# Squared-ReLU attention feeding a conv-gated FFN on one core: the FFN starts one block later, and the weight preparation is spread wider

## The chip, the cores and the metric

The kernel runs on one core of one Trainium2 chip. The metric is the device time of one execution in microseconds (us); lower is better. Three runs of the kernel before gave 1623.33, 1624.53 and 1624.59 us, so its time is the median, 1624.53 us.

## What is computed

```python
scores = (z @ z.T) / S                      # per batch, S = 3136, z is [S, 64]
x = u * (np.maximum(scores, 0) ** 2 @ v)    # u, v: [4, 3136, 256]
h = np.maximum(x @ w_in, 0)                 # w_in: [256, 1024]
conv = conv_w[0]*h[t-1] + conv_w[1]*h[t] + conv_w[2]*h[t+1]   # along the sequence
out = (h * sigmoid(conv)) @ w_out           # w_out: [1024, 256]
```

The three weight arrays arrive as float64; the rest is float32.

## The kernel before, in words

**Blocks and slots.** The queries are cut into 28 blocks (4 batches of 7) of 448 columns. A block goes over the 3136 keys of its batch in 25 slots, one per tile of 128 keys; the last tile is half a tile. So there are 700 slots. What each engine is to do in slot k stands in a table `ev[k]`, in six classes (PRE, MID, VEC, POST, PE0, PE1), and the loop at the end of the kernel walks the slots and issues each class in turn. Every engine carries out its own instructions in the order in which they were issued.

**Attention.** In slot k the kernel issues `attend(k)` (six matmuls: two halves dc of the output, three products each because values are split in a high and a low part; four matmuls in the half tile), and ahead of it `scores(k+4)` (two matmuls), `relu(k+3)` on ACT with `square(k+3)` on DVE, and `split_hi(k+2)` on ACT with `split_lo(k+2)` on DVE. Since z z^T is symmetric, some tiles are not computed again: POOL packs a computed tile (`part`), a DMA spills it to DRAM, and later blocks fetch it transposed (`fetch`, `join`); such a slot needs no scores and no square. The attention of one block is summed in two PSUM tiles `av0` and `av1`, one buffer each.

**From block to block.** At the first slot of block b+1, in class PRE, `gate_x` reads both `av` tiles of block b (DVE line L348 the first, ACT line L352 the second) and multiplies by u. The first attend matmul of block b+1 (L337) writes `av0` again and so waits for L348. One slot later `split_x` makes `xh` and `xl` (ACT L360, POOL) for the FFN.

**FFN.** The 1024 hidden columns of a block are eight chunks of 128. A chunk that starts in slot s issues `ffn_in` (six matmuls, L370 to L372, in class PE1, after attend and scores) in slot s, the ReLU in s+1, tap and first convolution step in s+2, the second step in s+3, sigmoid and gating in s+4, the split in s+5, and `ffn_out` (three matmuls each, L437 to L439, in class PE0, ahead of attend) in slots s+10 and s+11. Chunk f of block b starts at slot 25(b+1) + FS[f].

**Weights.** Each of the 16 blocks of 128x256 weights (eight of `w_in`, eight of `w_out`) is loaded as float64 words and rebuilt in float32 by `prep_w`, in five stages spread over four slots that start at WS[i]: two DVE instructions (L205, L209), two ACT and two DVE instructions (L216, L220), a POOL product (L222), a copy and a POOL subtraction. I call this one **weight set**. The three convolution weights go through the same stages once, starting in slot 5.

**Names in the rows.** `s`: scores in PSUM; `t`: ReLU output; `ah`, `al`: attention tile, high and low; `vh`, `vl`: values; `wr`, `wm`: raw and half-made weights; `ph`: FFN hidden tile in PSUM; `gh`, `gl`: gated hidden tile; `o`: FFN output in PSUM; `pl`, `tp`, `tj`: packed, fetched and joined tiles.

The line that sets the slots of the FFN before, and the one that reads it:

```python
FS = [2, 5, 8, 11, 15, 18, 21, 24]
...
            s = k0 + FS[f]          # k0 = (blk + 1) * NJ, NJ = 25
```

Of the kernel before, what the change touches and what calls it, by code (L numbers as in the profile page):

```python
# [8 lines left out]
F32 = mybir.dt.float32  # L9
F32R = mybir.dt.float32r  # L10
# [19 lines left out]
LD, LJ, LP, LX = 9, 5, 2, 1  # L30


FS = [2, 5, 8, 11, 15, 18, 21, 24]
RELU, TAP, ST1, ST2, SIG, GATE, GHI, OUT0, OUT1 = 1, 2, 2, 3, 4, 4, 5, 10, 11
EVAC = 12
XS = 1
# [2 lines left out]
C_RELU, C_TAP, C_XS, C_EV, C_V = 3, 1, 3, 3, 5  # L39


WS = [0, 8, 11, 17, 15, 21, 27, 22, 29, 34, 36, 38, 40, 45, 48, 53]
WST = [0, 1, 1, 2, 3]
W_E = ["GGGGGGGGGVGGGGGG", "AVVAAAAAVAAAAAAA"]
W_C = 5
# [11 lines left out]
def kernel(  # L57
# [11 lines left out]
    B, S, D = v.shape  # L69
# [3 lines left out]
    P = 128  # L73
    NB = 448
    QB = S // NB
    NJ = (S + P - 1) // P
    HALF = S - (NJ - 1) * P
    NBLK = B * QB
    NS = NBLK * NJ
    DC = D // P  # L80
    FC = DFF // P
# [5 lines left out]
    wk = ctx.enter_context(tc.tile_pool(name="wk", bufs=2))  # L87
# [15 lines left out]
    def at_slot(k):  # L103
        blk, i = divmod(k, NJ)
        return blk, *ent[blk % QB][i]
# [13 lines left out]
    def sub(eng, out, a, b):  # L119
        eng.tensor_tensor(out=out, in0=a, in1=b.bitcast(F32), op=ALU.subtract)  # L120
# [61 lines left out]
        return r[:, :, 0], r[:, :, 1]  # L182

    def load_w(what, i):
        t = wk.tile([P, 2 * D], F32, tag="wr", name="wr", bufs=3)
        raw = t.bitcast(U64)
        if what == "in":
            nc.sync.dma_start(
                out=raw.rearrange("p (a n) -> p a n", a=DC),
                in_=w_in[:, i * P : (i + 1) * P].rearrange("(a p) n -> p a n", p=P),  # L190
            )
        else:
            nc.sync.dma_start(out=raw, in_=w_out[i * P : (i + 1) * P, :])
        wst[what, i] = [t]
# [50 lines left out]
    def scores(k):  # L245
        blk, j, tr = at_slot(k)
        if tr:
            return

        tag = "ph" if k < NJ and k % 2 else "s"  # L250
        s = ps.tile([P, 512], F32, tag=tag, name="s", bufs=2)
        w = slice(j * P, (j + 1) * P)
        nc.tensor.matmul(s[:, :NB], lhsT=zhh[:, w], rhs=zq[blk], start=True, stop=False)  # L253
        nc.tensor.matmul(s[:, :NB], lhsT=zll[:, w], rhs=zq[blk], start=False, stop=True)  # L254
        sc[k] = s
# [88 lines left out]
    xh, xl = {}, {}  # L344
# [9 lines left out]

    def split_x(blk, engs):
        t = ut.pop(blk)
        xh[blk] = wk.tile([P, DC, NB], F32R, tag="xh", name="xh", bufs=1)
        xl[blk] = wk.tile([P, DC, NB], F32R, tag="xl", name="xl", bufs=1)
        for dc in range(DC):
            nc.scalar.copy(xh[blk][:, dc], t[:, dc])  # L360
            sub(engs[dc], xl[blk][:, dc], t[:, dc], xh[blk][:, dc])


    ph, hb, cc, gg, po = {}, {}, {}, {}, {}
# [13 lines left out]
    def width(blk):  # L378
        return NB + (2 if blk % QB == QB - 1 else 0)
# [63 lines left out]
    ob = {}  # L443

    def outs(blk):
        b, q = divmod(blk, QB)
        a, e = (1 if q == 0 else 0), NB + (1 if q == QB - 1 else 0)
        t = q * NB - 1
        return out[b, :, t + a : t + e].rearrange("(a p) s -> p a s", p=P), ob[blk][:, :, a:e]

    def evac(blk, end=False):
        e = width(blk)
        o = po.pop(blk)
        ob[blk] = r = wk.tile([P, DC, NB + 2], F32, tag="ob", name="ob")
        for dc in range(DC):
            if end and dc:
                nc.vector.tensor_copy(r[:, dc, :e], o[dc][:, :e])
            else:
                nc.scalar.copy(r[:, dc, :e], o[dc][:, :e])
            if end:  # L460
                dst, src = outs(blk)
                (nc.scalar if dc else nc.sync).dma_start(out=dst[:, dc], in_=src[:, dc])
# [14 lines left out]
    def at(slot, cls, fn, *args):  # L477
        ev[slot][cls].append((fn, args))


    for q in range(2, QB):
        s = (7 * q) // 2 - LA - 2
# [8 lines left out]
    for b in range(1, B):  # L491
        k0 = (b * QB - 1) * NJ
        for q in range(QB):
            s = k0 - (QB - 2 - q) * NJ + (12 if q % 2 == 0 else 4)
            if q == QB - 2:
                s = k0 + 6
            elif q == QB - 1:
                s = k0 + NJ + 6
            at(s - 4, POST, load_z, b, q)
            at(s, POST, prep_z, q)  # L500
        last = {j: i for i, (j, _) in enumerate(ent[QB - 1])}
        for j in range(0, NJ, 2):
            s = k0 + max(last[j] + 2, last.get(j + 1, 0) + 2, V0 + V1 * j // NJ)
# [2 lines left out]
    for blk in range(1, NBLK):  # L506
        at(blk * NJ - LA - 2, VEC, queries, blk)

    need = [(NJ + FS[f], "in", f) for f in range(FC)] + [(NJ + FS[f] + OUT0, "out", f) for f in range(FC)]
    for i, (_, what, f) in enumerate(sorted(need)):  # L510
        s = WS[i]
        at(s - 4, POST, load_w, what, f)
        for n in range(5):
            at(s + WST[n], POST, prep_w, n, what, f, *(E[x[i]] for x in W_E))
# [5 lines left out]
    for blk in range(NBLK - 1):  # L520
        k0 = (blk + 1) * NJ
        at(k0, C_GATE, gate_x, blk, G)
        at(k0 + XS, C_XS, split_x, blk, (G, G))
        for f in range(FC):
            s = k0 + FS[f]
            at(s, POST, ffn_halo, blk, f)
            at(s, PE1, ffn_in, blk, f)
            at(s + RELU, C_RELU, ffn_relu, blk, f)
            at(s + TAP, C_TAP, ffn_tap, blk, f)
            at(s + ST1, C_ST1, ffn_conv, blk, f, 1)  # L530
            at(s + ST2, C_ST2, ffn_conv, blk, f, 2)
            at(s + SIG, C_SIG, ffn_sig, blk, f)
            at(s + GATE, C_G, ffn_gate, blk, f, G)
            at(s + GHI, C_HI, ffn_hi, blk, f, A)
            at(s + GHI, PE1, ffn_lo, blk, f, G)
            at(s + OUT0, PE0, ffn_out, blk, f, 0)
            at(s + OUT1, PE0, ffn_out, blk, f, 1)
        at(s + EVAC, C_EV, evac, blk)
        at(s + EVAC + 2, POST, store, blk)
# [28 lines left out]
    with tc.manual_schedule():  # L568
# [12 lines left out]
        for k in range(-LA, max(ev) + 1):  # L581
            e = ev[k]
            run(e[PRE])
            if 0 <= k + LS < NS:
                split_hi(k + LS)
                split_lo(k + LS)
            run(e[MID])
            if 0 <= k + LT < NS:
                relu(k + LT)
                square(k + LT)  # L590
            run(e[VEC])
            run(e[POST])
            if 0 <= k + LD < NS:
                fetch(k + LD)
            if 0 <= k + LJ < NS:
                join(k + LJ)
            if 0 <= k + LP < NS:
                part(k + LP)
            if 0 <= k + LX < NS:
                spill(k + LX)  # L600
            run(e[PE0])
            if 0 <= k < NS:
                attend(k)
            if k + LA < NS:
                scores(k + LA)
            run(e[PE1])
# [41 lines left out]
```

## Time and profile before

| | |
|---|---|
| median of three runs | 1624.53 us |
| the profiled execution | 1625.38 us |
| its span in the profile | 1623.4 us |
| PE busy | 1585.0 us, 98%, 7656 matmuls |
| PE weight loads | 1441.2 us, 89% |
| ACT busy | 1262.5 us, 78% |
| DVE busy | 1161.0 us, 72% |
| POOL busy | 1125.4 us, 69% |

An engine's busy time is the union of its instructions' times. Matmuls overlap each other in the records (one lasts about 365 ns, the next starts after some 200 ns), so a PE that is busy without a break can still have gaps between starts that are longer than needed. The count of matmuls in a stretch, set against its length, tells that; the rows below have both.

### The profile page before, as it was taken

To read this page: it belongs to the slowest core of one execution; us is meant where nothing else is said; L and a number is where in the kernel's file an instruction comes from. 1 tells how busy PE (TensorE), PEld (TensorE's weight loads), DVE (VectorE), ACT (ScalarE), POOL (GpSimd) and SP (SyncE) were. 2 spreads that over 40 slices of the span, in tenths; PEclk is the share of its full clock that TensorE was granted. 3 is DMA by queue.
4 is the path that set the end of the run, shared out by engine and by line. 5 is a ranking of instruction groups with operands and counts; after the bars stand their busy time and mean duration, and the time that the engine had idled before them with its cause. 6 is when DMAs were issued, how large, how long until landed. Compare 5 with 4: busy or idle time off the path is not lost.

```text
span 1623.4 us, 24961 instructions
## 1 busy us (share of the span) xinstructions
PE 1585.0 (98%) x7656; PEld 1441.2 (89%) x7656; DVE 1161.0 (72%) x1952; ACT 1262.5 (78%) x2562; POOL 1125.4 (69%) x1473
## 2 busy tenths in 40 slices
PE   7788999999999999999999999999999999999998
PEld 6677899999999989999999998999999999999997
DVE  7998767666777767666777776766677777766666
ACT  6677778788877777788877777778887777787886
POOL 7876667778765666778685666776877566677772
PEclk9899999999999999999999999999999999999999
DMA  6453455456424435555453344555644334445540
GB/s 196 126 158 81 111 120 112 103 117 141 134 80 132 107 93 123 111 111 117 120 152 94 100 124 103 110 115 105 139 116 136 97 97 106 108 97 111 117 103 23
DMA packets 384486, 184.59 MB, mean 114 GB/s; under 512 B 275296, under 2 KB 383328, under 8 KB 384352
## 3 DMA queue, kind: packets, MB, share of 16 engines
q1 hardware_dynamic: 384208, 182.77, 46.2%
q8 instruction: 60, 0.98, 0.3%
q14 instruction: 74, 0.61, 0.1%
q10 hardware_dynamic: 144, 0.23, 0.0%
HBM read 36.59 MB, written 80.28 MB: 72 GB/s over the span
## 4 chain that ended last, share of the span: by engine, by line
PE 86%; ACT 5%; DVE 4%; issue 3%; POOL 1%; DMA 1%; POOLq 0%; SPq 0%; ACTq 0%; DVEq 0%
PE av L337 15%; PE av L338 15%; PE av L339 15%; PE ph L370 5%; PE ph L372 5%; PE o L439 5%; PE ph L371 5%; PE o L437 5%; PE s L253 5%; PE o L438 5%; PE s L254 5%; DVE al L120 1%; ACT t L304 1%; DVE ph L406 1%; ACT xh L360 1%
## 5 line engine op out<-in xcount | busy, mean ns | idle before, releaser
L120 DVE TENSOR_TENSOR al<-s,ah 128x448 fp32r<-128x448 f32 x672 | 418.8, 623 | 232.4 <-ACT ah L314 162.1
L337 PE MATMUL av<-ah,vl 128*128 128x448 f32 x1344 | 495.8, 369 | 13.7 <-POOL vl L120 9.4
L338 PE MATMUL av<-ah,vh 128*128 128x448 f32 x1344 | 494.5, 368 | 0.0
L339 PE MATMUL av<-al,vh 128*128 128x448 f32 x1344 | 493.5, 367 | 0.0
L309 DVE TENSOR_TENSOR s<-s,t 128x448 f32<-128x448 f32 x412 | 259.7, 630 | 210.2 <-ACT t L304 210.0
L296 POOL COPY tj<-tp 128x896 uint16<-128x896 uint16 x288 | 349.3, 1216 | 1.0 <-DMA tp<-dq 1.0
L316 ACT CAST ah<-s 128x448 fp32r<-128x448 f32 x412 | 220.1, 534 | 138.0 <-DVE s L309 136.0
L304 ACT ACTIVATE t<-s 128x448 f32<-128x448 f32 x412 | 224.8, 546 | 115.0 <-PE s L254 107.5
L406 DVE SCALAR_TENSOR_TENSOR ph<-hb,cw,ph 128x448 f32<-128x448 f32 (+1 forms) x448 | 305.1, 681 | 3.3 <-POOL gl L120 1.9
L120 POOL TENSOR_TENSOR gl<-c,gh 128x448 fp32r<-128x448 f32 (+1 forms) x220 | 256.2, 1165 | 59.9 <-ACT gh L123 57.4
L270 POOL COPY pl<-t 128x896 uint16<-128x896 uint16 x312 | 290.5, 939 | 3.0 <-DMA dq<-pl 2.2
L337 PEld LDWEIGHTS av<-ah,vl 128*128 128x128 f32 x1344 | 254.2, 189 | 40.8 <-POOL vl L120 12.3
L339 PEld LDWEIGHTS av<-al,vh 128*128 128x128 f32 x1344 | 254.1, 189 | 21.4 <-DVE al L120 0.2
L338 PEld LDWEIGHTS av<-ah,vh 128*128 128x128 f32 x1344 | 254.3, 189 | 20.5
L395 POOL COPY halo<-hb 128x2 f32<-128x2 f32 x192 | 37.1, 193 | 294.0 <-ACT hb L393 293.8
L253 PE MATMUL s<-zq,zhh 128*128 128x448 f32 x412 | 157.5, 382 | 18.7 <-DVE al L120 9.5
L314 ACT ACTIVATE ah<-tj 128x448 fp32r<-128x448 f32 x288 | 166.2, 577 | 1.6
L370 PE MATMUL ph<-xh,wih 128*128 128x448 f32 x448 | 164.4, 367 | 1.1 <-DVE c L420 0.6
L439 PE MATMUL o<-gl,woh 128*128 128x448 f32 (+1 forms) x448 | 164.3, 367 | 0.9 <-POOL gl L120 0.9
L437 PE MATMUL o<-gh,wol 128*128 128x448 f32 (+1 forms) x448 | 164.6, 367 | 0.0
L438 PE MATMUL o<-gh,woh 128*128 128x448 f32 (+1 forms) x448 | 164.2, 366 | 0.0
L372 PE MATMUL ph<-xl,wih 128*128 128x448 f32 x448 | 164.1, 366 | 0.0
(79 smaller groups left out, 2367.3 us busy)
## 6 DMA issues: line engine op xcount, KB each, us to landing
dq<-pl SPq DMA_DIRECT2D x252, 224.0 KB, 2.3
ut<-in_u_dram SPq DMA_DIRECT2D x28, 448.0 KB, 4.2
vst<-in_v_dram SPq DMA_DIRECT2D x48, 256.0 KB, 3.2
dq<-pl SPq DMA_DIRECT2D x84, 112.0 KB, 2.4
out_dram<-ob SPq DMA_DIRECT2D x20, 448.0 KB, 3.4
zt<-in_z_dram SPq DMA_DIRECT2D x28, 224.0 KB, 3.2
tp<-dq SPq DMA_TRANSPOSE x288, 3.3
wr<-in_moe_w_in_dram SPq DMA_DIRECT2D x8, 256.0 KB, 3.5
```

What stands on the lines that cost most here:

```text
L120: eng.tensor_tensor(out=out, in0=a, in1=b.bitcast(F32), op=ALU.subtract)
L270: nc.gpsimd.tensor_copy(pl[k], rl.pop(k).bitcast(U16).rearrange("p (n h) -> p h n", h=2))
L296: nc.gpsimd.tensor_copy(tj[k].bitcast(U16).rearrange("p (n h) -> p h n", h=2), t)
L309: nc.vector.tensor_tensor(out=s, in0=s, in1=rl[k], op=ALU.mult)
L337: nc.tensor.matmul(o, lhsT=vl[:, j, d], rhs=h, start=first, stop=False)
L338: nc.tensor.matmul(o, lhsT=vh[:, j, d], rhs=h, start=False, stop=False)
L339: nc.tensor.matmul(o, lhsT=vh[:, j, d], rhs=l, start=False, stop=False)
L370: nc.tensor.matmul(o, lhsT=wih[:, dc, w], rhs=xh[blk][:, dc], start=(dc == 0), stop=False)
L406: nc.vector.scalar_tensor_tensor(out=c, in0=hb[blk, f][:, k : e + k], scalar=cw[:, f, k : k + 1], in1=c, op0=ALU.mult, op1=ALU.add,)
L437: nc.tensor.matmul(o, lhsT=wol[:, f, d], rhs=h, start=(f == 0), stop=False)
L438: nc.tensor.matmul(o, lhsT=woh[:, f, d], rhs=h, start=False, stop=False)
L439: nc.tensor.matmul(o, lhsT=woh[:, f, d], rhs=l, start=False, stop=(f == FC - 1))
```

## The change

The FFN no longer starts one block behind with its own eight starting slots in each block. All chunks but the last block's form one even series: chunk number i = 8b + f starts in slot 52 + floor(647 i / 215), which is every three slots with one more now and then. The first starts in slot 52 instead of 27, the last in slot 699 as before. So the FFN of block b lies 27 slots behind the end of that block's attention at first and 3 at the end. The weight sets start every 4.25 slots from slot 4 to slot 67, instead of at the hand-set slots 0 to 53. `xh` and `xl` get two buffers, the raw weights two instead of three, the output tile one instead of two, and scores go on using the idle `ph` buffers for odd slots until slot 50.

```diff
-FS = [2, 5, 8, 11, 15, 18, 21, 24]
+FLAG, FLAST = 27, 2
-WS = [0, 8, 11, 17, 15, 21, 27, 22, 29, 34, 36, 38, 40, 45, 48, 53]
+WS = [4 + 17 * i // 4 for i in range(16)]
-        t = wk.tile([P, 2 * D], F32, tag="wr", name="wr", bufs=3)
+        t = wk.tile([P, 2 * D], F32, tag="wr", name="wr", bufs=2)
-        tag = "ph" if k < NJ and k % 2 else "s"
+        tag = "ph" if k < NJ + FLAG - 2 and k % 2 else "s"
-        xh[blk] = wk.tile([P, DC, NB], F32R, tag="xh", name="xh", bufs=1)
-        xl[blk] = wk.tile([P, DC, NB], F32R, tag="xl", name="xl", bufs=1)
+        xh[blk] = wk.tile([P, DC, NB], F32R, tag="xh", name="xh", bufs=2)
+        xl[blk] = wk.tile([P, DC, NB], F32R, tag="xl", name="xl", bufs=2)
-        ob[blk] = r = wk.tile([P, DC, NB + 2], F32, tag="ob", name="ob")
+        ob[blk] = r = wk.tile([P, DC, NB + 2], F32, tag="ob", name="ob", bufs=1)
-    need = [(NJ + FS[f], "in", f) for f in range(FC)] + [(NJ + FS[f] + OUT0, "out", f) for f in range(FC)]
+    nf, first, last = (NBLK - 1) * FC, NJ + FLAG, (NBLK - 1) * NJ + FLAST + 22
+    def fs(blk, f):
+        return first + (last - first) * (blk * FC + f) // (nf - 1)
+    need = [(fs(0, f), "in", f) for f in range(FC)] + [(fs(0, f) + OUT0, "out", f) for f in range(FC)]
-            s = k0 + FS[f]
+            s = fs(blk, f)
```

**Place 1: DVE in slots 29 and 30, in block 1.** `al` is a low split, `s` a square, `wm` are weight instructions, `ph` the convolution and `c` the gating of an FFN chunk. Before:

```order
L120 TENSOR_TENSOR al<-s,ah 128x448
L309 TENSOR_TENSOR s<-s,t 128x448
L406 SCALAR_TENSOR_TENSOR ph<-hb,cw,ph 128x448
L205 TENSOR_SCALAR wm<-wr 128x256
L209 TENSOR_SCALAR wm<-wr 128x256
L120 TENSOR_TENSOR al<-s,ah 128x448
L406 SCALAR_TENSOR_TENSOR ph<-hb,cw,ph 128x448
L216 SCALAR_TENSOR_TENSOR wm<-wr,wm 128x256
L220 SCALAR_TENSOR_TENSOR wm<-wr,wm 128x256
```

and with the change (line numbers one higher):

```order
L121 TENSOR_TENSOR al<-s,ah 128x448
L310 TENSOR_TENSOR s<-s,t 128x448
L206 TENSOR_SCALAR wm<-wr 128x256
L210 TENSOR_SCALAR wm<-wr 128x256
L121 TENSOR_TENSOR al<-s,ah 128x448
L217 SCALAR_TENSOR_TENSOR wm<-wr,wm 128x256
L221 SCALAR_TENSOR_TENSOR wm<-wr,wm 128x256
```

The convolution steps are gone from block 1; the weight sets stand alone between the attention's splits and squares.

**Place 2: PE at the border of blocks 12 and 13.** `av` is the attention sum (the number is the buffer), `ph` an FFN input, `o` an FFN output. Before:

```order
L341 MATMUL av_8363<-ah,vl 128x448
L342 MATMUL av_8363<-ah,vh 128x448
L341 MATMUL av_8364<-ah,vl 128x448
L342 MATMUL av_8364<-ah,vh 128x448
L370 MATMUL ph<-xh,wih 128x448
L371 MATMUL ph<-xh,wil 128x448
L372 MATMUL ph<-xl,wih 128x448
...
L437 MATMUL o_8677<-gh,wol 128x448
L438 MATMUL o_8677<-gh,woh 128x448
L439 MATMUL o_8677<-gl,woh 128x448
L337 MATMUL av_9017<-ah,vl 128x448
```

and with the change:

```order
L438 MATMUL o_8288<-gh,wol 128x448
L439 MATMUL o_8288<-gh,woh 128x448
L440 MATMUL o_8288<-gl,woh 128x448
L342 MATMUL av_8230<-ah,vl 128x448
L343 MATMUL av_8230<-ah,vh 128x448
L342 MATMUL av_8231<-ah,vl 128x448
L343 MATMUL av_8231<-ah,vh 128x448
L338 MATMUL av_8891<-ah,vl 128x448
L339 MATMUL av_8891<-ah,vh 128x448
L340 MATMUL av_8891<-al,vh 128x448
```

Between the last attend matmul of block 12 and the first of block 13 stood nine FFN matmuls; now nothing stands there. Counted in the same way over the whole order, the matmuls between the two at the borders of blocks 1|2 to 26|27 were 9 or 11 everywhere. With the change they are 9 or 11 at eight borders, 5 at five (2|3, 11|12, 14|15, 18|19, 21|22), 3 at four (5|6, 8|9, 15|16, 24|25), 2 at four (6|7, 9|10, 16|17, 25|26) and 0 at five (1|2, 3|4, 12|13, 19|20, 22|23). At 0|1 they are 2 in both.

## Rows read from the trace of the kernel before

**Rows 1.** The page: the span in 40 equal slices; busy tenths of PE, and the granted clock of TensorE in tenths.
```profile
PE   7788999999999999999999999999999999999998
PEclk9899999999999999999999999999999999999999
```

**Rows 2.** Busy time by stretch. The stretches are the time ahead of the first attend, block 0, block 1, block 2, blocks 3 to 26, block 27 with the tail, and last a stretch of block 2 without a break. Columns: length in us, then busy us (and count) of PE, PEld, DVE, ACT, POOL, then granted clock, DMA share, GB/s.
```profile
0.00:9.09 9.09, 3.56 (x9) 2.36 (x9) 3.13 (x7) 4.49 (x8) 3.66 (x7) 1.00 0.70 195
9.09:71.52 62.43, 49.47 (x198) 41.26 (x196) 54.98 (x89) 41.62 (x91) 51.98 (x56) 0.86 0.61 181
71.52:135.99 64.47, 56.02 (x265) 48.98 (x266) 58.97 (x105) 49.31 (x108) 46.49 (x64) 0.99 0.46 124
135.99:197.15 61.16, 60.02 (x280) 54.71 (x281) 44.72 (x76) 44.64 (x92) 39.66 (x54) 0.95 0.37 99
197.15:1540.39 1343.24, 1338.95 (x6539) 1225.35 (x6538) 945.79 (x1590) 1061.87 (x2146) 941.03 (x1228) 1.00 0.47 113
1540.39:1623.40 83.01, 76.95 (x370) 68.55 (x368) 53.37 (x90) 60.59 (x121) 42.60 (x67) 1.00 0.29 66
160.69:173.25 12.56, 12.56 (x64) 11.64 (x62) 9.20 (x16) 10.33 (x22) 9.48 (x13) 1.00 0.44 130
```

**Rows 3.** Timeline of DVE in slots 0 and 1, without FFN and without weights: start us, length us, instruction, and in brackets the idle time before it and what ended it.
```profile
8.32 0.62 DVE L120 TENSOR_TENSOR al<-s,ah 128x448 fp32r<-128x448 f32 x1 [0.60 <-ACT ah L316]
8.86 0.62 DVE L309 TENSOR_TENSOR s<-s,t 128x448 f32<-128x448 f32 x1
10.08 0.62 DVE L120 TENSOR_TENSOR al<-s,ah 128x448 fp32r<-128x448 f32 x1 [0.60 <-ACT ah L316]
10.62 0.62 DVE L309 TENSOR_TENSOR s<-s,t 128x448 f32<-128x448 f32 x1
```

**Rows 4.** Groups of DVE instructions in block 0 (9.09 to 71.52): the four of a weight set. Columns: count, busy us, mean ns of one, idle time before.
```profile
L220 DVE SCALAR_TENSOR_TENSOR wm<-wr,wm 128x256 f32<-128x256 uint32 x7 | 6.0, 855 | 0.0
L209 DVE TENSOR_SCALAR wm<-wr 128x256 uint32<-128x256 uint32 x7 | 5.6, 794 | 0.0
L216 DVE SCALAR_TENSOR_TENSOR wm<-wr,wm 128x256 uint32<-128x256 uint32 x7 | 5.2, 736 | 0.2
L205 DVE TENSOR_SCALAR wm<-wr 128x256 uint32<-128x256 uint32 x7 | 4.2, 605 | 0.0
```

**Rows 5.** The same groups in block 1 (71.52 to 135.99).
```profile
L205 DVE TENSOR_SCALAR wm<-wr 128x256 uint32<-128x256 uint32 x8 | 5.9, 734 | 0.0
L209 DVE TENSOR_SCALAR wm<-wr 128x256 uint32<-128x256 uint32 x8 | 5.4, 678 | 0.0
L216 DVE SCALAR_TENSOR_TENSOR wm<-wr,wm 128x256 uint32<-128x256 uint32 x8 | 5.0, 624 | 0.0
L220 DVE SCALAR_TENSOR_TENSOR wm<-wr,wm 128x256 f32<-128x256 uint32 x8 | 4.8, 598 | 0.0
```

**Rows 6.** Two of these instructions over the first 200 us: shortest, median and longest in ns.
```profile
L205 DVE TENSOR_SCALAR wm<-wr x16: 275/594/1264, 12.9 to 146.6; 128x256 uint32<-128x256 uint32 x16
L220 DVE SCALAR_TENSOR_TENSOR wm<-wr,wm x16: 411/420/1484, 15.9 to 149.7; 128x256 f32<-128x256 uint32 x16
```

**Rows 7.** Timeline at the border 0|1, with no FFN: last attend matmul, the gate on DVE, first attend matmul of block 1.
```profile
70.26 0.37 PE L342 MATMUL av<-ah,vh 128*128 128x448 f32 x1
70.76 0.61 DVE L348 SCALAR_TENSOR_TENSOR ut<-av,ut 128x448 f32<-128x448 f32 x1
71.52 0.44 PE L337 MATMUL av<-ah,vl 128*128 128x448 f32 x1 [0.48 <-DVE ut L348]
```

**Rows 8.** Timeline at the border 19|20, the same instructions, with the first and last of the nine FFN matmuls between them.
```profile
1145.05 0.36 PE L342 MATMUL av<-ah,vh 128*128 128x448 f32 x1
1145.24 0.37 PE L370 MATMUL ph<-xh,wih 128*128 128x448 f32 x1
1145.72 0.62 DVE L348 SCALAR_TENSOR_TENSOR ut<-av,ut 128x448 f32<-128x448 f32 x1
1146.87 0.37 PE L439 MATMUL o<-gl,woh 128*128 128x448 f32 x1
1147.08 0.37 PE L337 MATMUL av<-ah,vl 128*128 128x448 f32 x1
```

**Rows 9.** Timeline at the border 6|7: PE and DVE.
```profile
411.35 0.36 PE L342 MATMUL av<-ah,vh 128*128 128x448 f32 x1
411.67 0.62 DVE L309 TENSOR_TENSOR s<-s,t 128x448 f32<-128x448 f32 x1
411.81 0.47 PE L253 MATMUL s<-zq,zhh 128*128 128x448 f32 x1
412.20 0.68 DVE L406 SCALAR_TENSOR_TENSOR ph<-hb,cw,ph 128x448 f32<-128x448 f32 x1
412.79 0.62 DVE L348 SCALAR_TENSOR_TENSOR ut<-av,ut 128x448 f32<-128x448 f32 x1
414.15 0.36 PE L337 MATMUL av<-ah,vl 128*128 128x448 f32 x1
```

**Rows 10.** Timeline of PE at the border 1|2 and after it.
```profile
132.00 0.37 PE L439 MATMUL o<-gl,woh 128*128 128x448 f32 x1
135.99 0.71 PE L337 MATMUL av<-ah,vl 128*128 128x448 f32 x1 [3.63 <-DVE ut L348]
136.50 0.57 PE L338 MATMUL av<-ah,vh 128*128 128x448 f32 x1
136.88 0.57 PE L339 MATMUL av<-al,vh 128*128 128x448 f32 x1
...
141.35 0.52 PE L337 MATMUL av<-ah,vl 128*128 128x448 f32 x1
```

**Rows 11.** Timeline in the third slot of block 13: ACT splits x, and scores wait for their buffer.
```profile
756.23 1.04 ACT L360 CAST xh<-ut 128x448 fp32r<-128x448 f32 x2
757.70 0.37 PE L339 MATMUL av<-al,vh 128*128 128x448 f32 x1
757.79 0.62 DVE L120 TENSOR_TENSOR al<-s,ah 128x448 fp32r<-128x448 f32 x1 [1.68 <-ACT ah L314]
758.47 0.47 PE L253 MATMUL s<-zq,zhh 128*128 128x448 f32 x1 [0.40 <-DVE al L120]
```

**Rows 12.** All waits of PE in blocks 3 to 26 (197.15 to 1540.39): us in total, times, longest us.
```profile
PE s L253 <- DVE al L120: 3.4, 10, 0.5
```

## The prediction

> **What bounds the kernel now.** I read the page's slices first. PE is below nine tenths only in the first four of 40 and in the last, and its clock only in the second [rows 1]. The next view is busy time by stretch, cut at the first attend matmul of blocks 0 to 3 and 27 [rows 2]. A busy PE may hide gaps, so I compare length and count of matmuls. The last stretch of that view has 62 weight loads, thus 62 matmuls, in 12.56 us without a break: **0.2026 us each** is what a matmul costs at best. By it block 0 loses 62.43 - 196 x 0.2026 = 22.7 us, block 1 64.47 - 265 x 0.2026 = 10.8, block 2 61.16 - 280 x 0.2026 = 4.4, and blocks 3 to 26 together 1343.24 - 6539 x 0.2026 = 18.4, or 0.77 us a block. So nothing can be won on PE's work itself; what there is to win is 38 us in the first three blocks, and what there is to lose is the tightness of the 24 blocks behind them.
>
> What binds block 0 is a loop of ACT and DVE. Without weights, one square follows the last after 10.62 - 8.86 = 1.76 us, while eight matmuls need 1.62 us; in each turn DVE idles 0.60 us for ACT's high split [rows 3]. Weight sets must fit into that pause. Their four DVE instructions take 855 + 794 + 736 + 605 = 2.99 us on average in block 0 [rows 4] and 2.63 us in block 1 [rows 5], though the shortest L205 and L220 take 0.28 and 0.41 us [rows 6]. They are long where POOL is busy: it is busy for 51.98 of 62.43 us in block 0 and 46.49 of 64.47 us in block 1 [rows 2].
>
> **Block 0.** At 1.76 us a slot it would last 25 x 1.76 = 44.0 us; it lasts 62.4. The 18.4 us over that fall on seven weight sets and the set of convolution weights, 2.3 us each with all that they set off (late value splits, falls of the clock). The change leaves five sets (slots 4, 8, 12, 16, 21) and the convolution's: two fewer, **-4.6 us**. Bounds: 0, if POOL and not the sets holds the block; -8, if the sets cost more where two stand close together (slots 15 and 17, 21 and 22), which no longer happens. The mean is my choice, since the set in slot 5 now collides with the convolution's, and that speaks against the high end.
>
> **Block 1** loses its 72 FFN matmuls (eight inputs of six, eight half outputs of three) and so its filling: 193 remain, at best 39.1 us. It falls under the loop of block 0: 22 slots of 1.76 us, and three transposed ones at about the 1.2 us of their six matmuls, 42.3 us. Six weight sets start in it. One issues its next instruction some 0.08 us before the last ends [rows 3], so 2.63 us are about 2.2 us of queue; two pauses of 0.6 us take up 1.2, and 1.0 us is left per set, 6.0 us. The new query tile, a weight product and the gate at the border add about 1.5. Sum 49.8 us, of which 49.8 - 39.1 = 10.7 us are lost. Before it was 10.8: **-0.1 us**. What FFN and weights cost each other on DVE is saved, and what the FFN filled is left open. Bounds: sets free, -6; sets as dear as in block 0, 2.3 us, +8.
>
> **Block 2.** Its FFN starts in the third slot, beside five weight sets instead of one. Before, the border 1|2 alone stood 3.63 us still, since the gate L348 came behind four weight instructions, and the clock was at half for 14 starts after it [rows 10]. Now DVE has two slots without weights ahead of that gate, and no cover stands at the border: 1.06 us by the price below. Two slots without FFN with a set in them cost about 1.3, and DVE's lead over PE until the first outputs come in slot 62 about 1.7. Together 4.1 against 4.4: **-0.3 us**, bounds -3 and +3.
>
> **The borders.** Here the change takes something away that its description does not name. An attend matmul of a new block waits for the gate. At 0|1, where no FFN covers it, the first attend started 71.52 - 70.26 = 1.26 us after the last one [rows 7]. At 19|20 the gate was done at 1146.34, 1.29 us after the last attend began (1.11 at 0|1), and nobody noticed: nine FFN matmuls stood between, and PE went on at 1147.08 [rows 8]. With n matmuls of cover PE loses 1.26 - (n+1) x 0.2026 us: 0.04 at n = 5, 0.45 at 3, 0.65 at 2, 1.06 at 0, nothing at 9. By the order given with the change, the borders behind 1|2 have 5, 3, 2 and 0 at five, four, four and four places: 0.2 + 1.8 + 2.6 + 4.2 = **+8.8 us**. That is the low bound for a gate that starts at once. The high one is the border 6|7, where a square and a convolution step stood ahead of the gate and it ended at 413.41, 2.06 us after the last attend [rows 9]; with the 0.15 us from gate to matmul [rows 7] that is 2.2 us, and the same borders lose 0.98, 1.39, 1.59 and 2.0 us, 24.9 in all. A gate as at 19|20 would add 0.18 us at each, 3 us in all. I take the low one: with output matmuls now ahead of the half tile, PE gets there later than in rows 9, and DVE has the time to clear its queue.
>
> **What is given back there.** The 0.77 us a block are mostly score matmuls that wait for a buffer, because ACT does the gate and the two splits of x besides its own: 758.47 - 757.70 - 0.20 = 0.57 us in one place [rows 11], 411.81 - 411.35 - 0.20 = 0.26 in another [rows 9]. The view of waits counts only 3.4 us of them [rows 12], since a matmul's record runs on over the first 0.16 us of each gap. At the 17 loose borders PE either stands still anyway or has the long FFN slot sooner, so ACT catches up. I take half of it, 17 x 0.38 = **-6.5 us**; ends 0 and -13.
>
> **Nothing** comes of the buffers: a raw weight tile is read for the last time one slot after its set starts, and the load after the next is issued more than three slots later; the output tile has 24 slots. Code, DMA sizes and the tail (first and last slots of block 26's FFN, all of block 27) are as before.
>
> **Sum:** -4.6 - 0.1 - 0.3 + 8.8 - 6.5 = **-2.7 us**. The profiled execution took 1625.38 us, 0.85 above the median of the runs; -2.7 on the median of 1624.53 is **1621.8 us**.
>
> **Rivals.**
> - *The gates come late.* DVE's queue holds a square and a convolution step when the last attend ends, as at 6|7 [rows 9]: +24.9 instead of +8.8, so 1638; with some borders of each kind about 1634. For it: with 17 borders of short slots DVE gets less time per slot. Against it: the border 19|20, where the gate started 0.67 us after the last attend did, of which that matmul itself took 0.36 [rows 8]. It decides where the gate starts over 1 us after the last attend's start (1.44 us at 6|7). Slower.
> - *The clock falls in block 1.* After 3.63 us of standstill the starts were 0.37 us apart instead of 0.20, for 14 of them: 5.36 us where 2.84 would do, 2.5 us lost [rows 10]. In block 1, with PE idle in small pieces, the clock stayed at 0.99 [rows 2]. Four falls in the bare slots would cost 10 us and give 1632. The Trainium skill ("TensorE: Matmul & The Clock Gate", section "HAM oscillation — how this bites in real kernels") says that idle gaps between bursts of matmuls put the array back to half its clock time after time. The fall in rows 10 agrees with it; that the small gaps of block 1 caused none leaves it a low chance here.
> - *The weight sets become free in block 1.* Without the FFN's splits POOL has pauses; were all four instructions as short as the shortest [rows 6], a set would fit into two pauses, and 6 us more are saved: 1616. The Trainium skill ("SBUF — State Buffer", section "Who interferes with whom") says that such a DVE instruction and one of GpSimd lock each other out of a shared pair of ports for a whole instruction. By that rule the price falls with POOL's work, as rows 4 and 5 show in part (2.99 and 2.63 us).
>
> **How the numbers follow.** My forecast, early gains of 2 to 8 us and borders that net 0 to +5, gets 0.45 and covers 1617 to 1627. Late gates get 0.20, the clock 0.08, free sets 0.27. About 3.2 us, 0.2%, is what a measurement here can tell from no change. Faster by more is below 1621.3: all of the free sets and about 0.14 of the forecast, 0.41. Slower, above 1627.8, is the two other rivals, 0.28. The same is the rest, 0.31. The range that leaves out 2 in 10 goes from 1613 (free sets with a better block 0) to 1634; the forecast's own is 1617 to 1627.
>
> **What would show it.** By the same count of matmuls: block 0 near 58 us; block 1 near 50 us with 193 matmuls; block 2 at a loss near 4 us; blocks 3 to 26 with starts of L338 at the five bare borders about 1.26 us after the last L343, and those at the nine-matmul borders as before. The forecast is wrong if block 1 takes over 55 us or under 45, or if the bare borders show 2 us or none; the DVE row of L349 tells which. If the gaps at the score matmuls stay at 0.77 us a block, the term given back was none.

## The result: 22 us slower, and the profile after

The changed kernel took 1645.95 us (median of 4 runs, 1642.82 to 1648.20) against 1623.93 us before (4 runs, 1622.82 to 1624.59): 1.0136 times as long, 95% interval 1.0124 to 1.0148. The forecast was 1621.8, and the range ended at 1634. The profiled execution is the shortest of the four, 1642.82 us, with a span of 1641.0; that of the kernel before (1625.38) is longer than its median. So the traces, 17.6 us apart, show 4.4 us less than the medians. The mean granted clock was 0.994 in the profiled execution and 0.990 to 0.992 in the three longer ones, so falls of the clock like the one shown below are a likely cause of the rest; there is no trace of those three.

Busy time by stretch, cut as in [rows 2]: ahead of the first attend, blocks 0, 1 and 2, blocks 3 to 26, block 27 with the tail (us, then busy us and count of PE, PEld, DVE, ACT, POOL, clock, DMA share, GB/s):

```profile
0.00:9.12 9.12, 3.79 (x9) 2.57 (x10) 3.36 (x7) 4.49 (x8) 3.66 (x7) 1.00 0.61 171
9.12:71.59 62.47, 49.70 (x198) 40.43 (x196) 54.41 (x82) 39.99 (x87) 50.08 (x54) 0.89 0.61 175
71.59:120.27 48.68, 40.07 (x190) 35.20 (x191) 40.87 (x77) 32.60 (x72) 33.52 (x38) 1.00 0.58 152
120.27:183.63 63.36, 56.74 (x263) 50.03 (x264) 51.15 (x86) 45.87 (x97) 41.49 (x59) 0.97 0.42 105
183.63:1556.67 1373.04, 1358.86 (x6633) 1243.57 (x6632) 980.01 (x1615) 1076.23 (x2181) 957.04 (x1252) 1.00 0.46 111
1556.67:1641.00 84.33, 77.23 (x370) 68.47 (x368) 54.07 (x90) 60.42 (x121) 43.05 (x67) 1.00 0.30 64
```

Length less 0.2026 us for each matmul (196 in block 0) gives the loss, in us:

| | block 0 | block 1 | block 2 | blocks 3 to 26 | block 27, tail |
|---|---|---|---|---|---|
| before [rows 2] | 22.7 | 10.8 | 4.4 | 18.4 | 8.1 |
| after | 22.8 | 10.2 | 10.1 | 29.2 | 9.4 |
| change forecast | -4.6 | -0.1 | -0.3 | +2.3 | 0 |
| change measured | +0.1 | -0.6 | +5.7 | +10.8 | +1.3 |

Two entries make the result. The larger sits in blocks 3 to 26, but not at their borders. PE's waits there (us in total, times, longest), to be set beside [rows 12]:

```profile
PE s L254 <- DVE al L121: 9.8, 8, 2.3
PE av L338 <- ACT ah L317: 2.8, 3, 1.1
PE av L338 <- DVE ut L349: 0.8, 2, 0.4
```

The score waits were ten short ones of at most 0.5 us; now there are long ones. All of those over 1 us stand in slot 20 of blocks 8, 11, 15 and 18 (counted within the block); counted by the starts of PE these four lose 9.0 us. This is the timeline of block 8 there: `gl` and `tj` are POOL's low split of an FFN chunk and its joining of a fetched tile, `zq` the next block's query tile, made once a block by `queries` in slot 19.

```profile
511.24 0.63 DVE L310 TENSOR_TENSOR s<-s,t 128x448 f32<-128x448 f32 x1 [0.97 <-ACT t L305]
511.74 1.17 POOL L121 TENSOR_TENSOR gl<-c,gh 128x450 fp32r<-128x450 f32 x1 [2.37 <-ACT gh L124]
511.78 1.41 DVE L150 CAST zq<-zhh 64x448 fp32r<-64x448 f32 x1
512.89 1.35 POOL L297 COPY tj<-tp 128x896 uint16<-128x896 uint16 x1
513.20 1.28 DVE L151 CAST zq<-zll 64x448 fp32r<-64x448 f32 x1
513.65 0.37 PE L340 MATMUL av<-al,vh 128*128 128x448 f32 x1
514.51 0.69 DVE L407 SCALAR_TENSOR_TENSOR ph<-hb,cw,ph 128x450 f32<-128x450 f32 x1
515.24 0.62 DVE L121 TENSOR_TENSOR al<-s,ah 128x448 fp32r<-128x448 f32 x1
515.91 0.59 PE L254 MATMUL s<-zq,zhh 128*128 128x448 f32 x1 [1.90 <-DVE al L121]
```

The first cast ends 0.28 us after `gl` (511.74 + 1.17 = 512.91), the second 0.24 us after `tj`. Behind them stand a convolution step and the value split `al`, and PE waits for that to free the scores' buffer: 515.91 - 513.65 - 0.20 = 2.06 us lost. Right behind this stall the granted clock stood at 0.50, the lower of its two levels (1.2 and 2.4 GHz), for 3.41 us, which cost about half of that time, 1.7 us more:

```profile
516.11:519.52 3.41, 3.41 (x10) 3.02 (x10) 2.66 (x5) 1.87 (x4) 0.00 (x0) 0.50 0.20 67
```

Behind the three other stalls of 2 us and more it stayed at 1.00. In the same slot of the kernel before, of POOL's work only a copy of two columns (`halo`) and the first 0.02 us of `pl` overlap the casts:

```profile
519.39 0.38 DVE L149 CAST zq<-zhh 64x448 fp32r<-64x448 f32 x1
519.78 0.39 DVE L150 CAST zq<-zll 64x448 fp32r<-64x448 f32 x1
519.89 0.32 POOL L395 COPY halo<-hb 128x2 f32<-128x2 f32 x1 [3.42 <-ACT hb L393]
520.15 0.93 POOL L270 COPY pl<-t 128x896 uint16<-128x896 uint16 x1
```

Before, the casts always stood in the slot after a chunk's start (18, then 19). A series with a step of three in blocks of 25 slots shifts by one slot per block, so now every third block has them in a chunk's third slot, where the chunk before does its `gl`. Among those, the second and the fifth block of a batch also have a `tj` right behind it.

The smaller entry is block 2: five weight sets now stand beside the FFN, and a stall of the same kind (1.68 us, behind a cast of 1.19 us) stands in its slot 20. And block 0, with two sets fewer, lost as much as before.

### The profile page after: what moved, and what is told of

The parts are those of the page before. It is cut to its first block, busy times and chain, and to the rows that moved or that the text cites. A ratio compares the mean times of both kernels' runs of the same rounds, so it can differ in the third digit from the quotient of the medians.

```text
span 1641.0 us, 24940 instructions
## 1 busy us (share of the span) xinstructions
PE 1586.4 (97%) x7656; PEld 1440.3 (88%) x7656; DVE 1183.9 (72%) x1952; ACT 1259.6 (77%) x2562; POOL 1128.9 (69%) x1473
## 4 chain that ended last, share of the span: by engine, by line
PE 86%; DVE 6%; ACT 4%; issue 2%; POOL 0%; DMA 0%; POOLq 0%; DVEq 0%; ACTq 0%
PE av L338 15%; PE av L339 15%; PE av L340 15%; PE ph L371 5%; PE ph L373 5%; PE ph L372 5%; PE o L438 5%; PE o L440 5%; PE o L439 5%; PE s L254 5%; PE s L255 5%; DVE al L121 2%; DVE s L310 1%; ACT ah L317 1%; DVE ph L407 1%
## 5 line engine op out<-in xcount | busy, mean ns | idle before, releaser
L338 PE MATMUL av<-ah,vl 128*128 128x448 f32 x1344 | 496.2, 369 | 15.9 <-POOL vl L121 10.1
L372 PE MATMUL ph<-xh,wil 128*128 128x448 f32 x448 | 164.2, 367 | 0.0
```

Source lines behind the costliest of these rows:

```text
L338: nc.tensor.matmul(o, lhsT=vl[:, j, d], rhs=h, start=first, stop=False)
L372: nc.tensor.matmul(o, lhsT=wil[:, dc, w], rhs=xh[blk][:, dc], start=False, stop=False)
```

## Experiments

Kernels are compared with runs of the kernel before on the same chip, whose median lay between 1623.2 and 1623.7 us throughout.

### The casts moved to another slot

```diff
-        at(blk * NJ - LA - 2, VEC, queries, blk)
+        s = blk * NJ - LA - 2
+        while s >= first and s - 1 not in starts:   # starts: all fs(blk, f)
+            s -= 1
+        at(s, VEC, queries, blk)
```

> The changed kernel, but the next block's query tile is cast one or two slots earlier where that is needed, so that it always falls into the slot after an FFN chunk's start; it stays on DVE. Theory 1 (the two casts last 1.3 to 1.4 us each instead of 0.38 when they stand in the third slot of an FFN chunk, beside POOL's low split of the chunk before; convolution and value split behind them come late, and PE waits in slot 20): the waits of the score matmuls in slot 20 of blocks 8, 11, 15 and 18 (2.06 + 2.50 + 2.00 + 2.44 us) and of 14 and 21 (0.6 each) go, blocks 3 to 26 lose about 19 us instead of 29.2, and the kernel comes out some 10 us faster than the changed one, near 1636. Rival (the loss in blocks 3 to 26 is the price of the even series of FFN chunks and of the bare borders, wherever the casts stand): blocks 3 to 26 still lose 27 to 30 us, the stalls turn up one or two slots earlier, and the time is within 3 us of the changed kernel's.

1631.18 us, 1.0041 of before (1.0027 to 1.0055): 14.8 us less than the changed kernel. Blocks 3 to 26 take 1359.86 us for 6633 matmuls and lose 16.0 us. PE's waits there:

```profile
PE av L338 <- ACT ah L317: 2.9, 3, 1.1
PE av L338 <- DVE ut L349: 0.8, 2, 0.4
PE s L254 <- DVE al L121: 0.6, 2, 0.3
```

Theory 1 holds, with more gained than it said (16.0 us lost instead of some 19), and the rival falls: with the even series and the bare borders untouched, these blocks lose less than in the kernel before. Single casts still meet POOL: the longest first one took 1.25 us and the longest second one 1.43, and no score wait is longer than 0.3 us.

### The casts on ACT

```diff
-        nc.vector.tensor_copy(t[LO], zhh[LO, c].bitcast(F32))
-        nc.vector.tensor_copy(t[HI], zll[HI, c].bitcast(F32))
+        nc.scalar.copy(t[LO], zhh[LO, c].bitcast(F32))
+        nc.scalar.copy(t[HI], zll[HI, c].bitcast(F32))
```

> The changed kernel with the two query casts on ACT instead of DVE, in the same slot. Theory 1 (DVE's casts are slowed by POOL's work at the same time): on ACT they last about 0.4 us each with no long ones among them, the four waits of 2 us in slot 20 go (about -10 us), and ACT's 0.8 us more in one slot of each block costs 0 to 0.4 us a block, up to 11 us: 1636 to 1646. Theory that the casts are slow wherever they are done because they read the key tile that PE reads: they last over 1 us on ACT too, and nothing is won, 1646 or above. Rival (series and borders): stalls stay in slot 20 of blocks 8, 11, 15 and 18, and the time does not fall.

1633.91 us, 1.0062 (1.0047 to 1.0077). This is less than the 1636 to 1646 expected. Blocks 3 to 26 lose 1363.45 - 6633 x 0.2026 = 19.6 us, and the long score waits are gone:

```profile
PE s L254 <- DVE al L121: 2.1, 7, 0.6
```

One cast each, shortest, median and longest in ns, here, and then in the changed kernel:

```profile
L150 ACT CAST zq<-zhh x27: 550/554/566, 58.3 to 1535.5; 64x448 fp32r<-64x448 f32 x27
```

```profile
L150 DVE CAST zq<-zhh x27: 374/429/1408, 59.3 to 1544.0; 64x448 fp32r<-64x448 f32 x27
```

So it is DVE beside POOL, not the tile that is read: on ACT all 27 last alike, and the slot is the same. In block 8 of this run `gl` comes only after the casts, but 21 of the 54 casts on ACT stand beside a POOL instruction of 0.7 us or more and are no longer for it, as here in block 3:

```profile
226.14 1.16 POOL L121 TENSOR_TENSOR gl<-c,gh 128x448 fp32r<-128x448 f32 x1 [0.23 <-ACT gh L124]
227.22 0.56 ACT L150 CAST zq<-zhh 64x448 fp32r<-64x448 f32 x1
```

### The kernel before with the casts put into the bad slot

```diff
-FS = [2, 5, 8, 11, 15, 18, 21, 24]
+FS = [2, 5, 8, 11, 14, 17, 21, 24]
```

> The kernel before, with the starts of two FFN chunks of each block one slot earlier (14 and 17 for 15 and 18), so that the query casts in slot 19 stand in the third slot of a chunk in every block; nine matmuls still cover every border. Theory 1: in the blocks whose position in the batch is that of blocks 8, 11, 15 and 18 of the changed kernel (second and fifth of seven, 7 or 8 of 27 blocks) PE waits some 2.2 us in slot 20, in the first of a batch some 0.6 us: 18 us more, about 1642. Rival (the query casts have nothing to do with it): within 4 us of the kernel before, 1620 to 1628.

1656.46 us, 1.0201 (1.0186 to 1.0216): 32.8 us slower, more than expected. Gaps of 1.9 to 2.4 us stand in slot 20 of ten blocks, in the third of a batch too. The casts, and PE's waits in blocks 3 to 26:

```profile
L149 DVE CAST zq<-zhh x27: 374/719/1377, 56.6 to 1558.4; 64x448 fp32r<-64x448 f32 x27
```

```profile
PE s L253 <- DVE al L120: 23.1, 20, 2.2
```

The ten stalls lose some 21 us of the 27.5 us that these blocks lose more than in the kernel before. Behind four of them (blocks 8, 9, 15 and 16) the granted clock stood at 0.50 for 3.41 us, at up to 1.7 us more each. Two chunks moved by one slot cost half as much again as the whole change. The direction is settled from both sides: the delay of the FFN isn't needed for the loss, and its removal isn't needed for the cure. A kernel with these starts and the casts out of the way was not run.

### The weight sets of the kernel before

The changed kernel with `WS` of before and three raw buffers.

> The changed kernel with the weight sets of the kernel before (its list of slots, three raw buffers; a table warm-up writes to another tile to make room), so only one set stands in block 2 beside the FFN, and block 1, without FFN, has eight. Theory 2 (a set that stands beside an FFN chunk's convolutions costs PE about 1 us, one in block 1 about as much as its pauses leave): block 2 loses about 5 us instead of 10.3, block 1 about 12 instead of 10.2, block 0 as before 22.8: 3 to 4 us faster than the changed kernel. Rival (block 2 loses its time because the FFN is new there and its border bare, not by the sets): block 2 still loses 9 to 11 us, and the time is that of the changed kernel or 2 us above.

1651.98 us, 1.0175 (1.0160 to 1.0190). Block 2 lost 60.39 - 262 x 0.2026 = 7.3 us, about 3 less, but block 1, with its eight sets, 16.3, six more, and blocks 3 to 26 35.3. Expected was a gain; theory 2 missed what eight sets cost block 1. In the first three blocks the old slots cost some 2.6 us more than the wider spread, by one trace each. The six more in blocks 3 to 26, where no set stands, are not the sets': the stalls have the same lengths, but the granted clock stood at 0.50 for 3.41 us behind three of them instead of one (from 519.44, 925.63 and 1099.70), and blocks 15 and 18, with the two new falls, lost 3.1 us more. The rest is spread over the blocks and isn't settled.

The next kernels all have the casts moved as in the first experiment ("moved casts" below), and differ in the weight sets.

### Who holds block 0

The five sets of block 0 with product and last subtraction on DVE instead of POOL (not shown here: `prep_w` takes the engine of the subtraction as one more argument):

```diff
-W_E = ["GGGGGGGGGVGGGGGG", "AVVAAAAAVAAAAAAA"]
+W_E = ["VVVVVGGGGVGGGGGG", "AVVAAAAAVAAAAAAA"]
+W_S = "VVVVVGGGGGGGGGGG"      # engine of the last subtraction, was POOL
```

> The changed kernel with the query casts in the slot after a chunk's start, and with the five weight sets of block 0 done on DVE alone: the product and the last subtraction, 732 and 737 ns on POOL, move to DVE. Theory A, the one of the prediction (a set costs block 0 what it adds to DVE's queue): two more DVE instructions per set make block 0 some 5 x 1.0 = 5 us longer, loss 27 to 28 us instead of 23. Theory B (POOL holds block 0, PE waits there for the low values vl): 5 x 1.47 = 7.3 us of POOL's work and its waits for ACT and DVE go, and block 0 loses 15 to 20 us; PE's waits for vl, 10 us, fall by half.

1632.08 us, 1.0053 (1.0033 to 1.0072); block 0 lost 63.25 - 39.71 = 23.5 us. Both theories miss. PE's waits for `vl` fell from 11.2 to 7.4 us, and its waits for DVE's splits rose from 2.5 to 5.7: work taken from the one engine shows up on the other.

All sets after block 0, and then all ahead of block 2:

```diff
-WS = [4 + 17 * i // 4 for i in range(16)]
+WS = [26 + 33 * i // 10 for i in range(16)]
```

> As the kernel with the moved query casts, with all weight sets after block 0: one every 3.3 slots from slot 26 to 75, eight in block 1 and eight in block 2. Theory A (2.3 us a set on DVE's queue in block 0): block 0 loses 23 - 5 x 2.3 = 11.5 us. Theory B (POOL holds it, and of POOL's work the sets are 7.3 us of 50): it loses 14 to 19. In block 1, at about 3 us a set as the eight sets of the old list suggested (6.2 us for two more), the loss is 17 instead of 11; in block 2, three sets more at 0.75 us as the same run suggested, 13 instead of 10.6: 1628 to 1634 in all. If a set next to FFN chunks costs 2 us or more, block 2 loses 16 or more and it is 1635 or slower.

```diff
-WS = [4 + 17 * i // 4 for i in range(16)]
+WS = [3 * i for i in range(16)]
```

> As the kernel with the moved query casts, with all weight sets ahead of block 2: one every three slots from slot 0 to 45, nine in block 0 and seven in block 1. If block 0 hardly feels the number of sets (seven and five cost the same, 22.7 and 22.8 us), it loses 22 to 24 us; theory A says 23 + 4 x 2.3 = 32. Block 1, one set more: 11 to 14. Block 2 without a set beside the FFN: 6 to 7.5 us instead of 10.6, if the sets are what makes it dear; 10 or more, if the FFN's start itself does. Sum by the first of each: 1627 to 1631; by the second: 1637 or more.

1632.28 us, 1.0057 (1.0037 to 1.0077), and 1630.59 us, 1.0052 (1.0036 to 1.0068). Blocks 0, 1 and 2 with the moved casts, with late sets (block 0 alone), and with early ones:

```profile
8.98:71.81 62.83, 48.43 (x198) 39.25 (x196) 54.26 (x81) 39.37 (x86) 49.77 (x53) 0.92 0.59 175
71.81:121.55 49.74, 42.41 (x191) 36.93 (x191) 40.54 (x76) 32.75 (x73) 33.38 (x37) 0.94 0.57 148
121.55:185.18 63.63, 58.78 (x262) 51.71 (x263) 49.80 (x86) 46.38 (x98) 41.74 (x59) 0.94 0.42 105
```

```profile
9.04:60.38 51.34, 45.09 (x198) 38.45 (x196) 36.19 (x59) 34.44 (x73) 41.43 (x43) 0.97 0.64 188
```

```profile
8.89:75.92 67.03, 48.42 (x197) 38.95 (x196) 60.05 (x96) 43.18 (x97) 56.27 (x60) 0.92 0.59 172
75.92:129.31 53.39, 43.13 (x190) 37.59 (x191) 46.42 (x83) 34.72 (x78) 37.22 (x42) 0.93 0.49 139
129.31:184.91 55.60, 55.27 (x263) 50.25 (x264) 39.25 (x66) 40.47 (x82) 33.59 (x49) 0.97 0.45 106
```

Block 0 without a set lasts 51.34 us and loses 11.6, as theory A said (11.5); with five it loses 23.1, with nine 27.3 (theory A said 32). Block 2 without a set loses 55.60 - 263 x 0.2026 = 2.3 us instead of 10.5, so five sets cost 1.6 us each there, and the start of the FFN as such next to nothing. But the early sets' blocks 0 and 1 took back those 8.2 us, 4.2 and 3.7 of them. With late sets block 1 lost 17.0 us and block 2 11.9, near what was expected of a set's price there, and block 3, behind the last set in slot 75 and with one fall of the clock, lost 4.7 more than with the moved casts alone: together they took back what block 0 had gained.

### Which slots the sets stand in

```diff
-WS = [4 + 17 * i // 4 for i in range(16)]
+WS = [0, 8, 11, 15, 21] + [25 + 21 * i // 5 for i in range(11)]
```

> The changed kernel with the query casts in the slot after a chunk's start, and with the five sets of block 0 in slots 0, 8, 11, 15 and 21, which the kernel before uses too (it has two more, in 17 and 22, right behind two of these); all later sets as in the changed kernel, give or take one slot. If the two taken out were paid for one by one, at 1.6 us each ((22.7 - 11.6) / 7 over a block 0 without sets), block 0 loses 19 to 20 us and the kernel is some 3 us faster than with the sets in 4, 8, 12, 16 and 21. If two neighbours share one wait, so that the second of a pair is free, it loses 22 to 23, as with seven. If it is the slot that counts, and 4, 12 and 16 are dear ones, it falls to 16 to 18.

```diff
+WS = [5, 9, 13, 17, 21] + [4 + 17 * i // 4 for i in range(5, 16)]
```

> The same kernel with the sets of block 0 in slots 5, 9, 13, 17 and 21 instead of 4, 8, 12, 16 and 21, the rest untouched. POOL gets a pair of value tiles to split every second slot. If a set's price hangs on how its instructions fall between those, block 0 loses at least 2 us more or less than 23; if each set simply costs 2.3 us, 22.5 to 23.5.

1625.43 us, 1.0012 (1.0003 to 1.0022), and 1628.44 us, 1.0030 (1.0018 to 1.0042). Block 0 lost 19.5 us (59.21 us) and 20.2 us (59.91 us) instead of 23.1 with the same number of sets: the slot counts. The 19.5 is what the first of the three expectations said, but since the set's price was 2.3 us in the other slots, 1.6 us is no price of a set as such. The four DVE instructions of a set in block 0, after the change (the line of [rows 4]), and with the five slots of before:

```profile
L221 DVE SCALAR_TENSOR_TENSOR wm<-wr,wm 128x256 f32<-128x256 uint32 x5 | 6.4, 1280 | 0.0
L210 DVE TENSOR_SCALAR wm<-wr 128x256 uint32<-128x256 uint32 x5 | 6.2, 1241 | 0.0
L217 DVE SCALAR_TENSOR_TENSOR wm<-wr,wm 128x256 uint32<-128x256 uint32 x5 | 5.0, 1007 | 0.0
L206 DVE TENSOR_SCALAR wm<-wr 128x256 uint32<-128x256 uint32 x5 | 3.5, 701 | 0.0
```

```profile
L221 DVE SCALAR_TENSOR_TENSOR wm<-wr,wm 128x256 f32<-128x256 uint32 x5 | 4.6, 921 | 0.0
L210 DVE TENSOR_SCALAR wm<-wr 128x256 uint32<-128x256 uint32 x5 | 4.4, 880 | 0.0
L217 DVE SCALAR_TENSOR_TENSOR wm<-wr,wm 128x256 uint32<-128x256 uint32 x5 | 4.3, 855 | 0.2
L206 DVE TENSOR_SCALAR wm<-wr 128x256 uint32<-128x256 uint32 x5 | 2.8, 555 | 0.0
```

4.23 us a set against 3.21. Block 2 lost 59.19 - 262 x 0.2026 = 6.1 us in the first of these kernels, instead of 10.5, with its sets at 50, 54, 58, 62, 67 instead of 50, 55, 59, 63, 67; block 1, with two of its six sets one slot earlier, lost 13.8 instead of 11.3.

One trace of each kernel sets a limit to such prices. Three traces with the same five slots in block 0 lost 18.6, 19.5 and 19.9 us there, and three with the moved casts and the same slots in block 2 lost 8.9, 10.5 and 11.0 us, with granted clocks of 0.97, 0.94 and 0.93. So a price that rests on less than some 2 us of a block is an estimate.

### The best slots together

```diff
-WS = [4 + 17 * i // 4 for i in range(16)]
+WS = [0, 8, 11, 15, 21, 25, 29, 33, 38, 42, 46, 50, 54, 58, 62, 67]
```

> The delayed FFN with the query casts moved and the sets put together from the runs so far: block 0 as 0, 8, 11, 15, 21, block 1 with the changed kernel's six slots (25 to 46), block 2 as 50, 54, 58, 62, 67. If the price of a set is one of its slot, block 0 loses 19.5, block 1 11.3 instead of 13.8, block 2 6.1: 37 us against 38.0 in the kernel before, and 2.5 us less than with block 1's sets one slot earlier at two places, 1623. If block 1 depends on how block 0 ends rather than on its own slots, it loses 13 to 14 again: 1625.5.

```diff
-WS = [4 + 17 * i // 4 for i in range(16)]
+WS = [0, 8, 11, 15, 21, 25, 29, 33, 38, 50, 54, 58, 62, 66, 70, 74]
```

> The same with the two sets of slots 42 and 46 taken out of block 1, and seven sets in block 2 every four slots (50 to 74). A set in the bare block 1 cost 2 to 3 us (8 against 6: 17.0 and 11.3), one beside the FFN at these slots 0.7 us ((6.1 - 2.5) / 5). By these prices block 1 loses 6 to 8 us and block 2 7 to 8: 33 to 35 us for the first three blocks, 1620 to 1622, faster than the kernel before. If sets beside the FFN cost as in the changed kernel (1.6 us), or the last one at the border costs 4.7 as at slot 75, block 2 loses 10 to 13 and it is 1624 to 1627.

1623.05 us, 0.9997 (0.9989 to 1.0006), and 1623.56 us, 1.0002 (0.9993 to 1.0011). The first as expected, with these blocks 0 to 2 (18.6, 11.4 and 5.0 us lost):

```profile
8.95:67.24 58.29, 45.84 (x197) 38.35 (x196) 49.62 (x81) 39.05 (x86) 49.85 (x53) 0.97 0.60 182
67.24:117.14 49.90, 42.88 (x190) 37.05 (x191) 40.69 (x76) 32.69 (x73) 33.38 (x37) 0.94 0.56 150
117.14:175.20 58.06, 54.94 (x262) 49.24 (x263) 46.59 (x86) 45.80 (x99) 42.31 (x59) 0.99 0.50 115
```

The second misses its gain: with two sets fewer block 1 lost 10.2 us, only 1.2 less, and block 2 7.2. No version beats the kernel before by what can be measured. By medians, and in this order of steps, the change thus splits into 14.8 us for the casts, 1631.18 - 1623.05 = 8.1 us for the slots of the weight sets (the runs are from different chips, whose medians of the kernel before differ by 0.5 us), and about nothing for the delay of the FFN with the best slots found.

## Why the prediction was wrong, step by step

- **What bounds the kernel**: the reading held. The 24 later blocks had tightness to lose, and lost it; but the sentence led only to their borders.
- **Blocks 3 to 26** is the step that failed. The change part priced what the FFN's new slots do to the 17 borders and asked nothing of the work with a fixed place inside a block. The query casts weren't costed, nor named among "nothing"; moved against the FFN they cost 29.2 - 16.0 = 13.2 us in the traces (the four stalls 9.0, the fall of the clock behind one of them 1.7, the rest in smaller gaps), more than the distance to the end of the range. The sign was wrong for this reason first; with the casts moved the kernel was still 7.6 us slower than before (1631.18 against 1623.63), and the next cause is block 2.
- **The borders and what is given back**: +8.8 - 6.5 = +2.3 forecast; with the casts moved, 16.0 - 18.4 = -2.4. The price of the borders was too high, and that of late gates, the rival, even more so. At a bare border with DVE free, 12|13, the gate starts with the last attend and not 0.50 us behind it as at 0|1 [rows 7], and with a square and a convolution step ahead, 3|4, as in [rows 9], PE starts 1.44 us after the last attend, not 2.2. The changed kernel at 12|13 and at 3|4:

```profile
753.85 0.63 DVE L349 SCALAR_TENSOR_TENSOR ut<-av,ut 128x448 f32<-128x448 f32 x1 [0.20 <-PE av L343]
753.85 0.37 PE L343 MATMUL av<-ah,vh 128*128 128x448 f32 x1
754.62 0.44 PE L338 MATMUL av<-ah,vl 128*128 128x448 f32 x1 [0.40 <-DVE ut L349]
...
238.80 0.37 PE L343 MATMUL av<-ah,vh 128*128 128x448 f32 x1
238.89 0.68 DVE L407 SCALAR_TENSOR_TENSOR ph<-hb,cw,ph 128x448 f32<-128x448 f32 x1
239.48 0.62 DVE L349 SCALAR_TENSOR_TENSOR ut<-av,ut 128x448 f32<-128x448 f32 x1
239.65 0.53 ACT L317 CAST ah<-s 128x448 fp32r<-128x448 f32 x1
240.24 0.44 PE L338 MATMUL av<-ah,vl 128*128 128x448 f32 x1 [1.07 <-ACT ah L317]
```

  At 3|4 the profile puts the last wait down to ACT's high split, which ended 0.08 us after the gate (240.18 and 240.10); so there the gate alone does not set the time. The mechanism was right, the size wrong: 0.77 to 1.44 us from attend to attend at a bare border where 1.26 to 2.2 stood, and next to nothing lost (0.1 us in all) at the nine borders with 3 or 5 matmuls, where 2.0 stood. The give-back held. Counted start by start over blocks 3 to 26, each gap beyond 0.2026 us, what PE loses ahead of attend matmuls rose from 4.2 us to 8.7 with the moved casts, and what it loses ahead of score matmuls fell from 11.96 to 5.04: +4.5 and -6.9 where +8.8 and -6.5 were forecast.
- **Block 0**, -4.6: failed. The base of 1.76 us a slot, 44.0 us, is not reached without sets (51.34), so 2.3 us a set was too much for the old slots: (22.7 - 11.6) / 7 = 1.6. And the price isn't the set's own: in the new slots it is (23.1 - 11.6) / 5 = 2.3. Two sets fewer at 1.6 are -3.2, five at 0.7 more +3.5. The forecast's end of 0 was right, though not for its reason: POOL alone does not hold the block.
- **Block 1**, -0.1: right in size; 48.68 us where 49.8 was forecast, 190 matmuls for 193 (a ninth half output goes ahead of block 2's first attend). Its terms are not shown: the base of 1.76 a slot failed in block 0, 2.63 us less four times 0.08 are 2.3 us of queue and not 2.2, and four sets instead of six saved 1.2 us where 2.0 would follow, so some of this is luck. The clock stayed at 1.00 in this trace, but not in the same block of the kernels with the moved casts (0.94, 0.93 and 0.94 in the rows above; with the casts alone, 0.50 for 3.41 us from 84.94). So the rival of the falling clock is there in small, with one or two falls of at most 1.7 us each and not four of 2.5; it did not make this result. The free sets didn't come.
- **Block 2**, -0.3: failed by 6.0 us, outside its bound of +3. The sum had 1.3 us for two sets ahead of the FFN and nothing for the others beside it; they cost 1.6 us each where the change put them and 0.5 to 0.8 in other slots ((5.0 - 2.3) / 5 and (6.1 - 2.3) / 5), estimates from one trace each. Part of the 5.7 is the cast's stall of 1.68 us in slot 20; with the casts moved it was gone, but the granted clock was 0.94 instead of 0.97, and the block lost as much.
- **Tail**: 1.3 us were lost where nothing was forecast. PE waits 1.3 us in one place for DVE's gating of an FFN chunk, 0.6 us before; the kernel with the best slots has that wait too. Its cause was not tested.

## What to carry to other kernels

When a step of a periodic schedule gets another period, list everything that keeps its old place, and see in the trace which instructions of the other engines each one now meets; a loss of 2 us can come from two casts of 0.4. A mean duration taken in one arrangement is not a price: see how far shortest and longest are apart [rows 6], and what ran beside the long ones. Moving the weight sets out of block 0 took 11.5 us from it, and the blocks behind lost as much more (1632.28 us against 1631.18): a gain in one stage counts only with what the others then lose.

## What the runs showed of the hardware

The prediction put the spread of DVE's weight instructions [rows 6] down to POOL; for DVE's casts from SBUF to SBUF the traces show it one by one. 375 ns became 1408 ns, and such a cast ends 0.24 to 0.28 us after POOL's instruction that covers it, whichever that is (`gl` and `tj` above; in the same trace also `pl` and `vl`). The same cast on ACT took 550 to 566 ns in all 27 blocks. The Trainium skill ("SBUF — State Buffer", section "Who interferes with whom") says that a DVE instruction in a mode that uses both pairs of ports, which a cast can enter, contends with GpSimd (POOL in the rows): the first to issue holds the shared pair for its whole instruction, and the other one blocks. The trace agrees: `gl` starts at 511.74, the cast at 511.78, and the cast ends only after it. The long casts are not dear by themselves: in the last block of a batch in the kernel before they took up to 1.02 and 1.43 us without a gap on PE. Where they cost, both casts of a pair were long (1.28 to 1.41 us each in the four stalls) and a convolution step and a value split stood right behind them; that the cost hangs on how far DVE is ahead of PE is likely, and no run shows it apart.

The clock fell behind some stalls and not behind others of the same length: behind a stall of 2.06 us in block 8 of the changed kernel it stood at 0.50 for 3.41 us, and behind stalls of 2.50, 2.00 and 2.44 us in the same trace it stayed at 1.00. In the kernel with the old weight slots the stalls of blocks 15 and 18, just as long, did have the fall behind them. So a stall of 2 us can cost 3.7.
